# A transpose moved ahead of two weight transfers, and three fill steps moved across a score block: softcap attention followed by a maxout layer on one core

## The chip, the core and the metric

The kernel runs on one core of a Trainium2 chip. The metric is the device time of one execution in microseconds (us). Five engines of the core work side by side, each through its own queue of instructions in order: TensorE (PE in the profile, its weight loads apart as PEld), VectorE (DVE), ScalarE (ACT), GpSimd (POOL) and SyncE (SP). SP computes nothing here; it issues DMA transfers. The engines wait for one another through semaphores.

## The reference

For 8 batches of 12 heads, with 448 positions and a head size of 64, the reference computes softcap attention, and then feeds the result as 3584 rows of 768 numbers to a layer with two hidden products:

```
scores = (q @ k.T) / 8
scores = 30 * tanh(scores / 30)
attn   = exp(scores) / sum(exp(scores))        # the maximum is subtracted first
x      = attn @ v                              # 3584 x 768 after the heads are joined
out    = maximum(x @ w1, x @ w2) @ w_out       # w1, w2: 768 x 1024; w_out: 1024 x 768
```

The kernel doesn't subtract the maximum, since the cap bounds the scores. It uses maximum(a, b) = relu(a - b) + b: with wd = w1 - w2 it forms relu(x @ wd) @ w_out + x @ (w2 @ w_out). So w1 - w2 has to be computed once (`wd_sb`), and w2 @ w_out once (`wm_sb`).

## The kernel before

**Tiling.** Two heads make a pair, and there are N = 48 pairs. Three pairs are a group (g = 0 to 15, L = 3), the unit of loading. Two pairs are a quad (t = 0 to 23), the unit of attention. Pair i = 2t + p belongs to group i // 3. So quad 2 uses pairs 4 and 5 (group 1), quad 3 uses pairs 6 and 7 (group 2), quad 4 uses pair 8 (group 2) and pair 9 (group 3), and quad 5 uses pairs 10 and 11 (group 3).

**From q and k to scores.** For each group SP loads k and q (`load`, lines 117 to 145) into `kr` and `qr`; GpSimd casts them to bf16 into `kqf` (`cast`, lines 147 to 197; the last instruction of a cast of q is at line 190); then k and q must be turned so that the head dimension lies on the partitions. Pairs 0 to 5 are turned on TensorE. From group 2 on, `cross(g, n0, n1)` (line 290, its instruction at line 292) issues a DMA transpose of pairs n0 to n1 of the group on SP's queue, from `kqf` to `qkT`. `scores(t, p, last, js)` (line 302) multiplies for one pair: for each of three j two matmuls (line 318) into one PSUM tile, and then one tanh on ScalarE (line 319). The PSUM tiles are `s` (two buffers) or, where `last` is `v_psum` and for the last j, `v` (one buffer). `scores(t, 2)` does the 64 left-over keys of both pairs (line 315). `ex` is the exponential on ScalarE (line 324).

**Sums, values, the layer.** `total(t)` sums the exponentials on TensorE (lines 358, 362, 365), `values(t)` multiplies by v (lines 381, 387), and `normalize` scales on VectorE (line 402) into `xT`. When all quads of a batch are done, the layer for it (`moe`, line 406) is put into a list of fill work, `fill_q`: products with `wd_sb` (line 414), relu on VectorE (line 419), products with `wm_sb` (line 431) and `w_out` (line 434), copies (line 437) and stores. Ahead of these, the list holds the work that makes `wm_sb` (`turn_w2`, line 240; `premultiply`, line 249). `F(n)` (line 462) issues about n matmuls from the list, times `rate[0]`, which is 0.94 for quads 3 to 5 and 1.0 otherwise; a fraction left over is carried on. So the order of all work on every engine is written out by hand, with `F(n)` between the pieces of attention.

**wd_sb.** `load_w1(c, part)` (line 228, its instruction at line 232) loads half a block of 128 rows of w1 on SP's queue, 256 KB. Blocks 0 to 3 go to the `osb` buffers, blocks 4 and 5 to an `xT` buffer. `subtract(c, part, eng)` (line 234, its instruction at line 236) makes the block of `wd_sb`. Part 0 of blocks 0 and 1 and part 1 of block 5 are subtracted on VectorE, the rest on GpSimd. Part 0 serves the first four blocks of the hidden dimension, part 1 the last four.

**The stretch around the change.** Between lines 580 and 632 the program issues, on SP's queue: w1 part 0 of blocks 0 and 1, the transpose of the first pair of group 2 (pair 6), w1 part 0 of blocks 2 and 3, the main loads of k and q of pair 8, the transpose of pair 7, w1 part 0 of blocks 4 and 5, loads of group 3, the transpose of pair 8, w1 part 1 of all blocks, the transpose of pair 9 (`cross(3, 0, 1)`), loads for groups 3, 2 and 4, and the transpose of pairs 10 and 11 (`cross(3, 1, 3)`). A transpose waits on SP until the cast of its pair is done, and everything behind it in the queue waits with it. On GpSimd, in this order: the casts of pairs 6 and 7, half of a v cast, the subtractions of blocks 2 and 3 (part 0), the cast of pair 8, the subtractions of blocks 4 and 5 (part 0), the cast of pair 9, the subtractions of blocks 0 to 4 (part 1), and the casts of pairs 10 and 11.

The loop over the quads from 3 on (line 652) emits, for quad t, the scores of quad t + 1: `scores(t+1, 0, v_psum)` first, `scores(t+1, 1, v_psum)` in the middle (line 675), `scores(t+1, 2)` near the end, with `F(n)` and the additions of the exponentials on VectorE (`add`) between.

Of the kernel before, what the change touches and what calls it, by code (L numbers as in the profile page):

```python
# [10 lines left out]
def kernel(  # L11
# [216 lines left out]
    def load_w1(c, part):  # L228
        if c not in w1_in:
            w1_in[c] = opool.tile([P, DF], f32, name="osb") if c < OB else w1x[:, (c - OB) * DF : (c - OB + 1) * DF]  # L230
        cs = slice(part * (DF // 2), (part + 1) * (DF // 2))
        nc.sync.dma_start(out=w1_in[c][:, cs], in_=x_rows(moe_w1, c)[:, cs])

    def subtract(c, part, eng):
        cs = slice(part * (DF // 2), (part + 1) * (DF // 2))
        eng.tensor_sub(wd_sb[:, c, cs], w1_in[c][:, cs], w2b[part][:, c, :])
# [31 lines left out]
    def qkT_of(g):  # L268
        if g not in qkT:
            qkT[g] = stage.tile([P, L, 8, P], bf16, name="qkT")  # L270
        return qkT[g]
# [18 lines left out]
    def cross(g, n0=0, n1=L):  # L290

        nc.sync.dma_start_transpose(
            out=qkT_of(g)[:, n0:n1].rearrange("p n j c -> p (n j) c"),
            in_=kqf[g % 2][:, n0:n1].rearrange("p n j c -> p (n j c)"),
        )
# [6 lines left out]
    def scores(t, p, last=None, js=None):  # L302

        if (t, p) not in tanh:
            tanh[t, p] = att.tile([P, 2 * NJ, S], bf16, name="tanh")
        for j in js or range(NJ if p < 2 else 1):
            s = two_banks(last if last and j == NJ - 1 else s_psum)
            for m in range(2):
                i = 2 * t + (p if p < 2 else m)
                g = i // L  # L310
                k0 = qkT[g][:, i % L, :, :].rearrange("p j c -> p (j c)")
                o = Q0 + (64 * (i // NP % 2) if g >= NT else 0)
                qTn = k0[:, o : o + S]
                if p == 2:
                    nc.tensor.matmul(s[:, m, :S], k0[:, 3 * P : 4 * P], qTn)  # L315
                else:
                    r = slice(64 * m, 64 * m + 64)
                    nc.tensor.matmul(s[:, m, :S], k0[r, j * P : (j + 1) * P], qTn[r, :])  # L318
            nc.scalar.activation(tanh[t, p][:, 2 * j : 2 * j + 2, :], s[:, :, :S], AF.Tanh, scale=scale / cap)  # L319

    def ex(t, p):
        n = 2 * NJ if p < 2 else 2
        expo[t, p] = att.tile([P, n, S], bf16, name=f"expo{p}", bufs=2)
        nc.scalar.activation(expo[t, p], tanh[t, p][:, 0:n, :], AF.Exp, scale=float(cap))  # L324
# [6 lines left out]
    def add(t, ab, step):  # L331

        if t < NS or t >= NQ:
            return
        if t not in esum:
            esum[t] = att.tile([P, 4, S], bf16, name="esum")
        d = esum[t][:, 2 * ab : 2 * ab + 2, :]
        if step == 2:

            r = slice(64 * ab, 64 * ab + 64)  # L340
            d = esum[t][r, ab::2, :]
            nc.vector.tensor_add(d, d, expo[t, 2][r, :, :])  # L342
        elif step == 0:
            nc.vector.tensor_add(d, e_of(t, ab, 0), e_of(t, ab, 1))  # L344
        else:
            nc.vector.tensor_add(d, d, e_of(t, ab, 2))  # L346
# [5 lines left out]
    def total(t):  # L352

        ss = two_banks(s_psum)[:, 0, :]
        if t < NS:
            for j in range(NJ):
                for ab, h, r in HEADS:
                    nc.tensor.matmul(
                        ss[r, :S], ones[:, :32], e_of(t, ab, j)[:, h, :], start=(j == 0), stop=False
                    )  # L360
            for ab, h, r in HEADS:
                nc.tensor.matmul(ss[r, :S], ones2[:, h, :32], expo[t, 2][:, ab, :], start=False, stop=True)
        else:
            for ab, h, r in HEADS:
                nc.tensor.matmul(ss[r, :S], ones[:, :32], esum[t][:, 2 * ab + h, :], start=True, stop=True)  # L365
        st = att.tile([P, NB, 32], f32, name="st", bufs=1)
        nc.vector.transpose(st.rearrange("p b c -> p (b c)"), ss[:, :S])  # L367
        rs = att.tile([P, NB, 1], f32, name="rs", bufs=2)
        nc.vector.reciprocal(rs, st[:, :, 0:1])
        inv[t] = att.tile([P, S], f32, name="inv", bufs=2)  # L370
        nc.vector.transpose(inv[t].rearrange("p (b c) -> p b c", c=32), rs.to_broadcast([P, NB, 32]))  # L371

    def values(t):

        out = two_banks(v_psum)
        for u in range(2):
            ps = out[:, u, :]
            for j in range(NJ):
                for ab, h, r in HEADS:
                    g, n = divmod(2 * t + ab, L)  # L380
                    nc.tensor.matmul(  # L381
                        ps[r, :S], vp[g % 2][:, 2 * n + h, j, u::2], e_of(t, ab, j)[:, h, :],
                        start=(j == 0), stop=False,
                    )
            for ab, h, r in HEADS:
                g, n = divmod(2 * t + ab, L)
                nc.tensor.matmul(  # L387
                    ps[r, :S], vl[g % 2][:, n, 64 * h + u : 64 * h + 64 : 2], expo[t, 2][:, ab, :], start=False, stop=True
                )
        return out  # L390
# [9 lines left out]
    def normalize(t, ps):  # L400
        for u in range(2):
            nc.vector.tensor_mul(x_of(t, u), ps[:, u, :S], inv[t])  # L402
# [59 lines left out]
    def F(n):  # L462
        rate[1] += n * rate[0]
        while rate[1] >= 1 and fill_q:
            g = fill_q[0]
            if g is not rate[2]:
                rate[2] = g
                next(g)
            rate[1] -= 1
            try:  # L470
                next(g)
            except StopIteration:
                fill_q.pop(0)
        if not fill_q:
            rate[1] = 0.0
# [20 lines left out]
    def extra(i):  # L496
        for f, a in todo[i]:
            f(*a)
# [48 lines left out]
    def load_mains(g, n0, n1):  # L547
        for what in ("k", "q"):
            load(g, what, n0, n1, ("main",))
# [30 lines left out]
    for c in range(2):  # L580
        load_w1(c, 0)
    cross(2, 0, 1)
    for c in range(2, 4):
        load_w1(c, 0)
    load_mains(2, 2, 3)
    cross(2, 1, 2)
    for c in range(4, KC):
        load_w1(c, 0)
    load_mains(3, 0, 1)
# [62 lines left out]
    for t in range(3, NQ):  # L652
        i = 2 * t
        more = t + 1 < NQ
        rate[0] = 0.94 if t < 6 else 1.0
        if more:
            scores(t + 1, 0, v_psum)
        ex(t, 2)
        F(6)
        if t in crosses:  # L660
            cross(crosses[t])
        if t == 3:
            cast(nc.gpsimd, 3, "v")
        extra(i)
        F(2)
        add(t, 0, 0)
        F(3)
        if t == 3:
            subtract(5, 1, nc.vector)
        add(t, 0, 1)  # L670
        F(3)
        add(t, 1, 0)
        F(2)
        if more:
            scores(t + 1, 1, v_psum)
            ex(t + 1, 0)
        F(3)
        add(t, 1, 1)
        F(7)
        add(t, 0, 2)  # L680
        F(4)
        add(t, 1, 2)
        extra(i + 1)
        F(8)
        if more:
            scores(t + 1, 2)
            ex(t + 1, 1)
        total(t)
        normalize(t, values(t))
        if casts[t]:  # L690
            nc.gpsimd.tensor_copy(mark, inv[t][:1, :1])  # L691
            for g, what in casts[t]:
                cast(nc.gpsimd, g, what)
        if t % 3 == 2:
            fill_q.append(moe(t // 3))
        F(9)
# [34 lines left out]
```

## Time and profile before

The three runs of the kernel took 339.49, 339.53 and 340.0 us, a median of 339.53 us. The profiled execution has a span of 338.1 us.

| what | value |
|---|---|
| PE busy | 323.7 us (96% of the span) |
| ACT busy | 278.1 us (82%) |
| DVE busy | 229.0 us (68%) |
| POOL busy | 114.3 us (34%) |
| DMA moved | 61.78 MB, 183 GB/s on average |
| chain that ended last, by engine | PE 78%, DMA 12%, DVE 3%, ACT 3% |
| granted TensorE clock | full over the whole span |

How to read it: busy times are of one execution, and the engines overlap. The chain that ended last is followed back from the last instruction, at each step to whatever released it. A table of waits names for each waiting instruction what came last of the things it waited for. The timeline gives start and duration of each instruction, several of one kind merged (x4), and in brackets how long its engine sat idle before it and what ended that. For a DMA the duration in the timeline is that of its issue on SP's queue; when it landed is told apart. PE's ends are modelled, so merged neighbours can overlap by a tenth of a microsecond or two. Times below count from the start of the span.

### The profile page before, as it was taken

How to read it: one execution, taken by the hardware profiler on the slowest of the kernel's cores; microseconds unless marked ns; L12 is line 12 of the kernel's file. 1: busy time of each engine (PE TensorE's matmuls, PEld its weight loads, DVE VectorE, ACT ScalarE, POOL GpSimd, SP SyncE). 2: the span in 40 equal slices, each digit the busy share in tenths (PEclk: the TensorE clock that was granted, in tenths of full speed). 3: DMA queues.
4: the chain of work that ended last, by engine and by line, in shares of the span. 5: the costliest groups of instructions: out<-in, count | busy, mean ns of one | idle time of the engine just before them, and what ended most of it. 6: DMA issues, size and time to landing. Idle time of an engine off the chain costs nothing.

```text
span 338.1 us, 6876 instructions
## 1 busy us (share of the span) xinstructions
PE 323.7 (96%) x2721; PEld 163.8 (48%) x2722; DVE 229.0 (68%) x414; ACT 278.1 (82%) x243; POOL 114.3 (34%) x196
## 2 busy tenths in 40 slices
PE   4899989999999999999999999999999999999995
PEld 2555434455445454455445544445444554555563
DVE  4446865678787767768787576876886687874411
ACT  4999989999999999899989998999989999800000
POOL 8344698554323431440341344044034220000000
PEclk9999999999999999999999999999999999999999
DMA  7999999999997699568939699849955820012032
GB/s 221 188 237 280 264 241 293 261 257 237 214 311 156 189 233 282 134 158 188 315 96 221 87 263 292 176 100 240 295 107 137 211 95 2 0 48 93 2 93 93
DMA packets 106239, 61.78 MB, mean 183 GB/s; under 512 B 62816, under 2 KB 101088, under 8 KB 106208
## 3 DMA queue, kind: packets, MB, share of 16 engines
q1 hardware_dynamic: 102336, 58.21, 67.2%
q0 software_dynamic: 3872, 3.15, 6.1%
q8 instruction: 21, 0.34, 0.4%
q14 instruction: 10, 0.08, 0.1%
HBM read 42.47 MB, written 11.01 MB: 158 GB/s over the span
## 4 chain that ended last, share of the span: by engine, by line
PE 78%; DMA 12%; DVE 3%; ACT 3%; POOL 1%; issue 1%; SPq 1%; POOLq 0%; DVEq 0%
PE mm L434 22%; PE mm L414 20%; PE mm L431 16%; PE v L381 6%; PE s L318 6%; DMA kr<-in_k_dram 5%; DMA qkT<-kqf 3%; DMA kr<-in_moe_w_out_dram 2%; PE v L318 2%; DMA gT<-in_moe_w_dram 2%; PE v L387 2%; PE s L315 2%; PE s L365 2%; ACT expo L324 1%; ACT tanh L319 1%
## 5 line engine op out<-in xcount | busy, mean ns | idle before, releaser
L324 ACT ACTIVATE expo<-tanh 128x2688 bf16<-128x2688 bf16 (+1 forms) x72 | 140.3, 1950 | 0.2
L319 ACT ACTIVATE tanh<-s 128x896 bf16<-128x896 f32 x123 | 107.4, 915 | 13.7 <-PE s L318 11.0
L434 PE MATMUL mm<-wo_sb,gT 128*128 128x384 bf16 (+2 forms) x448 | 86.3, 327 | 0.0
L414 PE MATMUL mm<-xT,wd_sb 128*128 128x448 bf16 x384 | 78.4, 353 | 0.9 <-DVE gT L419 0.6
L431 PE MATMUL mm<-wm_sb,xT 128*128 128x384 bf16 (+2 forms) x335 | 65.5, 326 | 0.1
L437 DVE COPY osb<-mm 128x384 f32<-128x384 f32 (+2 forms) x56 | 31.1, 556 | 43.4 <-PE mm L434 42.8
L434 PEld LDWEIGHTS <-gT 128*128 128x128 bf16 x448 | 41.9, 98 | 35.9 <-issue 9.9
L414 PEld LDWEIGHTS <-wd_sb 128*128 128x128 bf16 x384 | 35.7, 98 | 40.4 <-issue 9.9
L419 DVE TENSOR_SCALAR gT<-mm 128x448 bf16<-128x448 f32 x64 | 39.6, 622 | 20.9 <-PE mm L414 18.4
L691 POOL COPY mark<-inv 1x1 f32<-1x1 f32 x17 | 3.0, 177 | 124.8 <-DVE inv L371 109.0
L431 PEld LDWEIGHTS <-xT 128*128 128x128 bf16 x336 | 32.0, 98 | 24.7 <-issue 4.1
L319 ACT ACTIVATE tanh<-v 128x896 bf16<-128x896 f32 x45 | 41.6, 925 | 0.0
L381 PE MATMUL v<-expo,vp 128*32 128x448 bf16 x576 | 35.9, 353 | 0.0
L318 PE MATMUL s<-qkT 64*128 64x448 bf16 x198 | 28.3, 363 | 3.6 <-DVE qkT L288 1.8
L402 DVE TENSOR_TENSOR xT<-v,inv 128x448 bf16<-128x448 f32 x48 | 27.7, 620 | 2.6 <-PE v L387 0.3
L346 DVE TENSOR_TENSOR esum<-esum,expo 128x896 bf16<-128x896 bf16 x40 | 26.9, 672 | 1.0
L367 DVE STREAM_TRANSPOSE st<-s 128x448 f32<-128x448 f32 x24 | 15.6, 648 | 16.7 <-PE s L365 12.7
L342 DVE TENSOR_TENSOR esum<-esum,expo 64x896 bf16<-64x896 bf16 x40 | 25.0, 625 | 1.2
L344 DVE TENSOR_TENSOR esum<-expo 128x896 bf16<-128x896 bf16 x40 | 25.8, 645 | 0.0
L318 PEld LDWEIGHTS <-qkT 64*128 64x128 bf16 x288 | 10.5, 95 | 25.7 <-issue 15.6
L381 PEld LDWEIGHTS <-vp 128*32 128x32 bf16 x576 | 15.8, 97 | 10.0 <-DVE vp L157 0.4
L185 POOL CAST kqf<-qr 128x1152 bf16<-128x1152 f32 (+2 forms) x17 | 17.0, 999 | 6.7 <-DMA qr<-in_q_dram 5.8
(68 smaller groups left out, 266.2 us busy)
## 6 DMA issues: line engine op xcount, KB each, us to landing
vr<-in_v_dram SPq DMA_DIRECT2D x14, 576.0 KB, 5.0
out_dram<-osb SPq DMA_DIRECT2D x20, 384.0 KB, 3.9
kr<-in_k_dram SPq DMA_DIRECT2D x12, 576.0 KB, 6.6
qr<-in_q_dram SPq DMA_DIRECT2D x12, 576.0 KB, 7.1
out_dram<-osb SPq DMA_DIRECT2D x14, 192.0 KB, 4.7
osb<-in_moe_w_dram SPq DMA_DIRECT2D x8, 256.0 KB, 4.2
gT<-in_moe_w_dram POOLq DMA_DIRECT2D x12, 128.0 KB, 9.4
wo_sb<-in_moe_w_out_dram POOLq DMA_DIRECT2D x4, 384.0 KB, 8.6
```

What stands on the lines that cost most here:

```text
L318: nc.tensor.matmul(s[:, m, :S], k0[r, j * P : (j + 1) * P], qTn[r, :])
L319: nc.scalar.activation(tanh[t, p][:, 2 * j : 2 * j + 2, :], s[:, :, :S], AF.Tanh, scale=scale / cap)
L324: nc.scalar.activation(expo[t, p], tanh[t, p][:, 0:n, :], AF.Exp, scale=float(cap))
L344: nc.vector.tensor_add(d, e_of(t, ab, 0), e_of(t, ab, 1))
L346: nc.vector.tensor_add(d, d, e_of(t, ab, 2))
L381: nc.tensor.matmul(ps[r, :S], vp[g % 2][:, 2 * n + h, j, u::2], e_of(t, ab, j)[:, h, :], start=(j == 0), stop=False,)
L402: nc.vector.tensor_mul(x_of(t, u), ps[:, u, :S], inv[t])
L414: nc.tensor.matmul(ps[:, :S], wd_sb[:, c, f * P : (f + 1) * P], x[:, c, cs], start=(c == 0), stop=(c == KC - 1))
L419: nc.vector.tensor_relu(g[f // FH][:, f % FH, cs], ps[:, :S])
L431: nc.tensor.matmul(ps, x[:, c, ts], wm_sb[:, c, hs], start=(c == 0), stop=False)
L434: nc.tensor.matmul(ps, g[f // FH][:, f % FH, ts], wo_sb[:, f, hs], start=False, stop=(f == FC - 1))
L437: nc.vector.tensor_copy(osb[:, hs], ps)
```

## The change

```diff
     for c in range(2):
         load_w1(c, 0)
     cross(2, 0, 1)
+    cross(2, 1, 2)
     for c in range(2, 4):
         load_w1(c, 0)
     load_mains(2, 2, 3)
-    cross(2, 1, 2)
     for c in range(4, KC):
         load_w1(c, 0)
     load_mains(3, 0, 1)
...
         add(t, 1, 0)
-        F(2)
+        F(2 if t > 3 else 5)
         if more:
             scores(t + 1, 1, v_psum)
             ex(t + 1, 0)
         F(3)
         add(t, 1, 1)
-        F(7)
+        F(7 if t > 3 else 4)
         add(t, 0, 2)
```

The first part moves the transpose of pair 7 on SP's queue: it is issued directly behind the transpose of pair 6, ahead of w1 part 0 of blocks 2 and 3 and of the main loads of pair 8, which each move one place back. It is meant to bring pair 7 to TensorE sooner. The second part concerns quad 3 alone, which is the fourth: three units of fill work are taken from behind the scores of pair 9 and put ahead of them. With the rate of 0.94 these are two matmuls in the instruction stream: two products of line 414 stand ahead of the six score matmuls of pair 9 that stood behind them. Nothing is added or removed: all engines have the same instructions as before, GpSimd in the same order.

## The prediction

> **What bounds the kernel now.** I read first the page's busy times, then the busy time by stretch, to find where TensorE has idle time at all, then TensorE's waits, then the timelines of the engines around the edit.
>
> Page, busy time by engine:
>
> ```profile
> PE 323.7 (96%) x2721; PEld 163.8 (48%) x2722; DVE 229.0 (68%) x414; ACT 278.1 (82%) x243; POOL 114.3 (34%) x196
> ```
>
> Busy time by stretch (start:end, length, then busy us of PE, PEld, DVE, ACT, POOL; clock, DMA share, GB/s):
>
> ```profile
> 46.00:67.00 21.00, 20.15 (x182) 9.38 (x180) 11.98 (x22) 19.28 (x16) 16.42 (x24) 1.00 1.03 256
> 67.00:130.00 63.00, 62.73 (x508) 31.04 (x509) 47.12 (x81) 61.51 (x55) 24.77 (x37) 1.00 0.94 231
> 130.00:330.00 200.00, 199.32 (x1567) 100.37 (x1567) 140.73 (x250) 157.43 (x137) 45.73 (x76) 1.00 0.59 150
> ```
>
> From 67 us to 330 us TensorE idles 0.27 + 0.68 = 0.95 us in all. Its work there is fixed, so the end is (the moment at which TensorE gets to its work of 67 us) + (a constant). Before that it has waits. Table of TensorE's waits from 30 us on (total, times, longest):
>
> ```profile
> PE s L318 <- DMA qkT<-kqf: 1.8, 2, 1.4
> PE mm L414 <- DVE gT L419: 0.6, 1, 0.6
> PE v L318 <- ACT tanh L319: 0.4, 1, 0.4
> ```
>
> The largest are two waits for a DMA transpose. TensorE's timeline says where:
>
> ```profile
> 44.96 0.55 PE L318 MATMUL s<-qkT 64*128 64x448 bf16 x4 [1.35 <-DMA qkT<-kqf]
> ...
> 57.92 0.37 PE L318 MATMUL v<-qkT 64*128 64x448 bf16 x2 [0.43 <-ACT tanh L319]
> ...
> 67.01 0.55 PE L318 MATMUL s<-qkT 64*128 64x448 bf16 x4 [0.42 <-DMA qkT<-kqf]
> ```
>
> By program order these are the scores of pair 7 (44.96, the transpose that the edit moves), of pair 9 (56.94, its third part 57.92) and of pair 10 (67.01, the transpose of pairs 10 and 11). The edit aims at the first. The question is whether the last one lets any of it through. SP's timeline shows the issues (start, duration of the issue):
>
> ```profile
> 35.49 2.20 SPq L292 DMA_TRANSPOSE qkT<-kqf  x1
> 37.74 1.04 SPq L232 DMA_DIRECT2D osb<-in_moe_w_dram  x2
> ...
> 39.87 1.34 SPq L292 DMA_TRANSPOSE qkT<-kqf  x1
> ...
> 46.31 1.26 SPq L292 DMA_TRANSPOSE qkT<-kqf  x1
> 47.62 2.86 SPq L232 DMA_DIRECT2D osb<-in_moe_w_dram  x4
> ...
> 60.72 3.12 SPq L292 DMA_TRANSPOSE qkT<-kqf  x1
> ```
>
> and GpSimd's timeline shows who waits for these:
>
> ```profile
> 41.35 2.27 POOL L236 TENSOR_TENSOR wd_sb<-osb,gT 128x512 bf16<-128x512 f32 x2 [2.00 <-DMA osb<-in_moe_w_dram]
> ...
> 45.99 0.29 POOL L190 CAST kqf<-qr 64x128 bf16<-64x128 f32 x1
> ...
> 51.85 4.49 POOL L236 TENSOR_TENSOR wd_sb<-osb,gT 128x512 bf16<-128x512 f32 x4 [1.38 <-DMA osb<-in_moe_w_dram]
> ...
> 60.30 0.40 POOL L190 CAST kqf<-qr 64x256 bf16<-64x256 f32 x1
> ```
>
> The reader is to see one chain through these rows. w1 part 0 of block 2, issued at 37.74, lands 3.5 us later (41.24); GpSimd, idle for 2.00 us, starts its subtractions at 41.35; behind them stands the cast of pair 8, done at 45.99 + 0.29 = 46.28; SP issues that transpose at 46.31 (its queue had been ready since 45.65); behind it stands w1 part 1, issued at 47.62, landing 4.1 us later; GpSimd, idle for 1.38 us, starts at 51.85, ends the casts of pairs 10 and 11 at 60.70; SP issues their transpose at 60.72; it lands 6.24 us later, at 66.96; TensorE starts pair 10 at 67.01. **The moment that sets the end hangs on the landing of w1 block 2**, and this is what the edit moves back.
>
> **The Trainium skill.** "DMA: Bandwidth & Descriptors", section "Queues, rings and completion order": SP owns one row of rings, and on each DMA engine descriptors are consumed in ring order. So what is issued first from SP is moved first; the trace fits: w1 block 2 landed at 41.24, behind the first transpose (35.49 + 4.3 = 39.8). "SBUF — State Buffer", section "Who interferes with whom": a VectorE instruction with two SBUF inputs and a GpSimd instruction that reads SBUF exclude each other. The trace agrees: VectorE's subtraction takes 0.70 us at 44.57 and 1.23 at 42.94 beside GpSimd's, and GpSimd's cast of k takes 0.50 us at 48.58 and 0.96 at 43.58. "TensorE: Matmul & The Clock Gate", "The mechanism": matmuls start and end in strict order; so fill behind waiting scores can't run, as the idle 1.35 us shows.
>
> **The change part by part.**
>
> *The transpose of pair 7 moves ahead.* Its cast ended at 37.42 and SP was free at 37.69, so it can issue at 37.74 instead of 39.87. The first transpose landed 4.3 us after its issue, the old place gave 5.04, and the third, on a quiet queue, 3.2. Thus it lands at 41 to 42.8. TensorE wants it at 44.96 - 1.35 = 43.61. I take the whole 1.35 us as gone, at this place.
>
> *Who profits.* ScalarE doesn't at first: the tanh of pair 7 started at 45.58, right behind an exponential that ended at 45.55, so PSUM tiles come free no sooner than 46.5, and `total(2)`, at 47.50 before, can't start before that. So 1.0 us of the 1.35 goes on, and ScalarE's wait for TensorE at 48.77 (1.47 us) shrinks by as much. On this side quad 3 runs 1.0 us ahead.
>
> *w1 blocks 2 and 3 and the loads of pair 8 move back* by one issue of a transpose. Transposes of one pair took 1.34, 1.26 and 1.29 us (the last at 51.59), and the first of all took 2.20. I take 1.3, with 2.2 as the upper bound. w1 block 2 then issues at 39.05; with the same 3.5 us behind a transpose in flight it lands at 42.55. GpSimd starts at 42.65 in place of 41.35. Queued behind the waiting subtraction are all casts of pairs 8 to 11. From 41.35 to 46.28 GpSimd needed 4.93 us, of which 2.27 (subtractions) + 1.9 (four casts, as at 48.58 to 50.47) = 4.17 is its own and 0.76 is exclusion by VectorE. VectorE's two subtractions stay near 43 to 45 us, so they still meet GpSimd. I take no recovery; a full one is the lower bound, 1.3 - 0.76 = 0.5. The loads of pair 8 move from 38.83 to about 40.15 and land 3.7 us later, before GpSimd wants them at 44.9: nothing.
>
> *On from there*, 1.3 us later all along: cast of pair 8 done 47.6 (SP waits longer in its place), w1 part 1 issued 48.9, subtractions from 53.15, casts of pairs 10 and 11 done 62.0, transpose issued 62.0, landed 68.25. The slack that the trace shows on the way (GpSimd's idle 1.38 us, SP's wait ahead of 60.72) is not slack of this chain: both wait for members of it. The loads of k and q for pairs 10 and 11 are issued at 52.92 and 54.04 in the same queue behind w1 part 1, so they shift too.
>
> *The fill moved ahead.* Pair 9's transpose was issued at 51.59 and took 5.0 us (56.6); now about 57.9. TensorE would be there at 56.94 - 1.0 = 55.9, with two products at 0.2 us each at 56.3. The two products cost nothing: they lie in this wait of 1.6 us. So TensorE starts pair 9 at 57.9, about 1 us later than before, and its lead is gone. Then it needs block 4 of `wd_sb` part 1, ready 57.96 + 1.3 = 59.3, for the second product behind the scores: some 0.4 us of wait. It reaches pair 10 at about 67.3, and waits for 68.25.
>
> *Sum.* Gone: 1.35 us at 44.96. New: 1.6 at pair 9, 0.4 at the product, and about 1.0 in place of 0.42 at pair 10. The start of pair 10 moves from 67.01 to 68.3, +1.3 us, and after that nothing is left to make it up. 339.5 + 1.3 = 340.8 us. By the bounds: +0.5 gives 340.0, +2.2 gives 341.7.
>
> **The rivals.**
>
> *No change (339.5).* w1 block 2 lands nearly as early, or the exclusion of GpSimd is gone by the shift, and pair 10's transpose lands where it did. For it: 0.76 us of exclusion that can vanish, and the DMA queue was held back by the 2.20 us issue at 35.49. Against: even then at least 0.5 us is left, by my count. TensorE's gain of 1.0 us ends in the wait at 67.
>
> *Faster.* The chain through GpSimd doesn't shift, and pair 10's transpose lands sooner than in 6.24 us (pair 9's took 5.0, pair 8's 3.2). Then up to the 1.0 us that passes ScalarE comes through: 339.5 - 1.0 = 338.5. For it: the 6.24 us are mostly queueing behind the v and k loads, which can fall otherwise. Against: those loads shift with the chain, and GpSimd waits for w1 at 41.35 with nothing between.
>
> *Slower by more.* The second transpose also takes 2.2 us to issue, back to back with the first: 341.7. This is the upper end of the likeliest case.
>
> **How the numbers follow.** The shifted chain: 0.62, of which a little falls under 0.2% (0.68 us), but some of the case of no change lies above it too. No change: 0.2. Faster: 0.18. So faster 0.19, same 0.21, slower 0.6. The range goes from 338.8, which leaves out the outer part of the faster case, to 341.8, the 2.2 us bound.
>
> **What would show it.** Right: TensorE's wait at pair 7 gone; the second transpose issued near 37.7; GpSimd's first w1 subtraction near 42.6 instead of 41.35; pair 8's transpose near 47.6; the transpose of pairs 10 and 11 near 62.0, and pair 10 on TensorE near 68.3, with a longer wait for the DMA. Wrong: GpSimd starting its subtractions before 41.9, or its cast of pair 8 ending by 46.3; or the transpose of pairs 10 and 11 landing before 66.9.

## The result, and the profile after

The changed kernel took 341.74 us (median of 6 runs, 340.36 to 342.63), beside 339.51 us of the kernel before (6 runs, 338.98 to 340.0): ratio 1.0062, 95% interval 1.0036 to 1.0087. It is slower by 2.2 us. The forecast was 340.8 us with a range up to 341.8. The views below are those shown of before, of an execution of the changed kernel with a span of 340.4 us and a time of 342.32 us.

The page, busy time by engine:

```profile
PE 323.8 (95%) x2722; PEld 163.5 (48%) x2722; DVE 229.8 (67%) x414; ACT 277.9 (82%) x243; POOL 114.0 (33%) x196
```

All engines do the same work as before. Busy time by stretch (start:end, length, busy us of PE, PEld, DVE, ACT, POOL; clock, DMA share, GB/s):

```profile
28.00:46.00 18.00, 17.42 (x207) 8.68 (x205) 15.08 (x26) 16.78 (x17) 12.00 (x23) 1.00 1.05 262
46.00:67.00 21.00, 18.89 (x174) 8.71 (x173) 11.25 (x20) 19.66 (x16) 17.17 (x28) 1.00 1.12 246
67.00:130.00 63.00, 61.12 (x499) 30.24 (x498) 46.39 (x79) 59.14 (x53) 24.46 (x37) 1.00 0.94 227
130.00:330.00 200.00, 199.37 (x1569) 99.94 (x1568) 141.90 (x252) 159.82 (x139) 46.36 (x79) 1.00 0.60 153
```

The stretches up to 46 us, first of the kernel before, then of the changed one:

```profile
0.00:28.00 28.00, 21.18 (x245) 12.39 (x246) 13.52 (x36) 23.34 (x21) 14.36 (x33) 1.00 1.08 225
28.00:46.00 18.00, 16.12 (x199) 8.31 (x198) 14.28 (x26) 16.54 (x17) 13.01 (x27) 1.00 1.06 270
...
0.00:28.00 28.00, 20.39 (x242) 12.18 (x243) 13.13 (x35) 22.55 (x21) 13.99 (x33) 1.00 1.07 223
```

The gain that was aimed at is there, but it is small: from 28 to 46 us TensorE is busy 1.30 us more than before (17.42, 16.12), and 0.79 us of this is work that this execution hadn't done yet at 28 us (20.39, 21.18). Some 0.5 us remain. From 46 to 67 us it does 1.26 us less than before (18.89, 20.15), and the next row loses 1.61 us more, since pair 10 now falls into it. After that nothing differs. TensorE's largest waits (total, times, longest), and where they are:

```profile
PE s L318 <- DMA qkT<-kqf: 1.6, 1, 1.6
PE s L318 <- ACT expo L324: 1.3, 1, 1.3
```

```profile
43.68 0.36 PE L318 MATMUL s<-qkT 64*128 64x448 bf16 x2
44.33 0.36 PE L318 MATMUL s<-qkT 64*128 64x448 bf16 x2 [0.28 <-ACT tanh L319]
...
58.15 0.55 PE L318 MATMUL s<-qkT 64*128 64x448 bf16 x4 [1.34 <-ACT expo L324]
...
64.31 0.75 PE L381 MATMUL v<-expo,vp 128*32 128x448 bf16 x12 [0.60 <-POOL vp L164]
...
69.40 0.55 PE L318 MATMUL s<-qkT 64*128 64x448 bf16 x4 [1.62 <-DMA qkT<-kqf]
```

Pair 7 (43.68, its second two matmuls at 44.33) no longer waits for its transpose. Pair 9 (58.15) and pair 10 (69.40) do. The wait at 58.15 is put down to an exponential of ScalarE, but SP issued that transpose at 52.92 and it landed 5.2 us later, at 58.1: the transpose was the real release. SP's timeline (start, duration of the issue):

```profile
34.67 1.34 SPq L292 DMA_TRANSPOSE qkT<-kqf  x1
36.63 2.40 SPq L292 DMA_TRANSPOSE qkT<-kqf  x1
39.08 1.06 SPq L232 DMA_DIRECT2D osb<-in_moe_w_dram  x2
...
44.47 0.61 SPq L136 DMA_DIRECT2D qr<-in_q_dram  x1
47.50 1.26 SPq L292 DMA_TRANSPOSE qkT<-kqf  x1
48.81 2.99 SPq L232 DMA_DIRECT2D osb<-in_moe_w_dram  x4
...
62.54 3.03 SPq L292 DMA_TRANSPOSE qkT<-kqf  x1
```

and GpSimd's:

```profile
42.45 2.72 POOL L236 TENSOR_TENSOR wd_sb<-osb,gT 128x512 bf16<-128x512 f32 x2 [3.76 <-DMA osb<-in_moe_w_dram]
...
47.18 0.29 POOL L190 CAST kqf<-qr 64x128 bf16<-64x128 f32 x1
...
52.96 4.49 POOL L236 TENSOR_TENSOR wd_sb<-osb,gT 128x512 bf16<-128x512 f32 x4 [1.28 <-DMA osb<-in_moe_w_dram]
...
59.76 0.82 POOL L185 CAST kqf<-kr 128x768 bf16<-128x768 f32 x1 [0.74 <-DMA kr<-in_k_dram]
```

The reader is to see the same chain as before, each link later: w1 issued at 39.08 (37.74 before), GpSimd at 42.45 (41.35), the transpose of pair 8 at 47.50 (46.31), GpSimd's second batch at 52.96 (51.85), the transpose of pairs 10 and 11 at 62.54 (60.72), pair 10 at 69.40 (67.01). From 45.08 to 47.50 SP's queue stands still, 2.42 us in place of 0.66. Behind that hole the DMA engines move less: in the row for 47 to 51 us (last two numbers: DMA share, GB/s) they moved 100 GB/s, and 211 in the same row of the kernel before, which stands second:

```profile
47.00:51.00 4.00, 4.00 (x58) 1.90 (x58) 2.68 (x6) 3.48 (x3) 3.73 (x8) 1.00 1.08 100
...
47.00:51.00 4.00, 4.00 (x58) 1.71 (x57) 2.61 (x6) 2.53 (x3) 3.29 (x7) 1.00 0.94 211
```

The share of 1.08 shows that the engines weren't empty over these 4 us. Only from 48 to 49 us is it low (0.37 at 73 GB/s; 1.30 at 215 before). From 49 to 51 us it is 1.61 at 106 GB/s, while the transpose of pair 8 was on its way; it landed 4.5 us after its issue (3.2 before).

### The profile page after: what moved, and what is told of

It is laid out like the page before. It is cut to its first block, busy times and chain, and to the rows that moved or that the text cites. A ratio compares the mean times of both kernels' runs of the same rounds, so it can differ in the third digit from the quotient of the medians.

```text
span 340.4 us, 6877 instructions
## 1 busy us (share of the span) xinstructions
PE 323.8 (95%) x2722; PEld 163.5 (48%) x2722; DVE 229.8 (67%) x414; ACT 277.9 (82%) x243; POOL 114.0 (33%) x196
## 4 chain that ended last, share of the span: by engine, by line
PE 75%; DMA 16%; DVE 3%; SPq 2%; POOL 2%; issue 1%; POOLq 0%; DVEq 0%
PE mm L434 21%; PE mm L414 19%; PE mm L431 16%; PE v L381 6%; PE s L318 5%; DMA qr<-in_q_dram 3%; DMA vr<-in_v_dram 3%; DMA gT<-in_moe_w_dram 2%; PE v L387 2%; PE v L318 2%; DMA kr<-in_moe_w_out_dram 2%; DMA qkT<-kqf 2%; PE s L315 2%; DMA xT<-in_moe_w_dram 2%; PE s L365 2%; DMA osb<-in_moe_w_dram 1%
```

## The experiments

The theory is the chain: the landing of w1 block 2, GpSimd's queue, SP's queue, the transpose of pairs 10 and 11, pair 10 on TensorE. The rivals: the moved fill costs the time; two transposes back to back cost it; or where w1 stands doesn't matter. The kernel before ran beside each experiment, with medians of 339.94 to 340.43 us, so ratios are compared.

**The two parts of the change, each alone.** The transpose moved, the fill as before:

> The transpose of pair 7 moved ahead as in the changed kernel, the fill left where it was. Theory (chain through the landing of w1 block 2 on GpSimd): the two products of fill lay in a wait, so this costs as much as the whole change: 341.7 us, pair 10 on TensorE near 69.4. Rival (the fill put ahead of pair 9 is what costs): 339.5 us or less.

Measured: 341.36 us, ratio 1.0046 (1.0030 to 1.0061). In the profiled execution pair 10 started at 67.96, not near 69.4. The fill moved, the transpose as before:

```diff
-        F(2)
+        F(2 if t > 3 else 5)
...
-        F(7)
+        F(7 if t > 3 else 4)
```

> The fill moved as in the changed kernel, the transpose left where it was. Theory: TensorE comes to pair 9 some 0.4 us later and loses its 0.43 us wait for the tanh there; it still waits for the transpose of pairs 10 and 11: 339.5 us (339.2 to 339.8). Rival (the fill is what costs): 341 us or more.

Measured: 339.94 us, ratio 0.9996 (0.9982 to 1.0009); the kernel before took 339.94 us beside it, so the window was missed by 0.1 us with no difference behind it. The fill does nothing that can be measured, and the moved transpose alone is slower. The intervals of the transpose alone and of the whole change overlap, so no difference between these two is shown. TensorE's timeline of the fill alone carries a second reading:

```profile
43.10 0.83 PE L318 MATMUL s<-qkT 64*128 64x448 bf16 x4
...
67.08 0.55 PE L318 MATMUL s<-qkT 64*128 64x448 bf16 x4 [1.67 <-DMA qkT<-kqf]
```

Here SP's queue has the old order, and pair 7 (43.10) doesn't wait at all. The 1.35 us at which the change aimed was that of one execution.

**w1 delayed alone.** The kernel before, with the two w1 parts one place back, behind the loads of pair 8. No transposes are adjacent, and pair 8's loads come earlier:

```diff
     cross(2, 0, 1)
+    load_mains(2, 2, 3)
     for c in range(2, 4):
         load_w1(c, 0)
-    load_mains(2, 2, 3)
     cross(2, 1, 2)
```

> The kernel before, with w1 blocks 2 and 3 put behind the two main loads of pair 8; the transpose of pair 7 keeps its place, no two transposes are adjacent, the fill is as before. w1 is issued some 0.95 us later. Theory: GpSimd's first subtraction near 42.3 in place of 41.35, pair 10's transpose issued 1 to 1.7 us later, the end at 340.5 to 341.5 us, with the wait of 1.35 us at pair 7 still there. Rival (adjacent transposes or fill cost the time): 339.5 us.

Measured: 341.60 us, ratio 1.0049 (1.0028 to 1.0069). The delay of w1 alone is enough (the time is 0.1 us above its window). SP's timeline and GpSimd's:

```profile
43.62 0.61 SPq L136 DMA_DIRECT2D qr<-in_q_dram  x1
46.65 1.26 SPq L292 DMA_TRANSPOSE qkT<-kqf  x1
...
61.63 2.97 SPq L292 DMA_TRANSPOSE qkT<-kqf  x1
```

```profile
41.59 2.72 POOL L236 TENSOR_TENSOR wd_sb<-osb,gT 128x512 bf16<-128x512 f32 x2 [3.27 <-DMA osb<-in_moe_w_dram]
```

The mark is the idle time of GpSimd, 3.27 us for w1, and SP's hole from 44.23 to 46.65, 2.42 us, as in the changed kernel. Two details missed: the wait at pair 7 was 0.22 us, not 1.35, and GpSimd's first subtraction started at 41.59, not near 42.3. Both are matters of the single execution, in which SP reached the transpose of pair 6 1.05 us sooner than in that of the kernel before (34.44, 35.49).

**More of the delay.** The changed kernel, w1 behind the loads of pair 8:

```diff
     cross(2, 0, 1)
     cross(2, 1, 2)
+    load_mains(2, 2, 3)
     for c in range(2, 4):
         load_w1(c, 0)
-    load_mains(2, 2, 3)
```

> The changed kernel, with w1 blocks 2 and 3 one place further back, behind the main loads of pair 8: the suspected delay grows from 1.3 to about 2.25 us, the transposes are as in the changed kernel. Theory: the end another 0.9 to 1.5 us later, 342.5 to 343.3 us. Rival (the adjacency of the transposes costs, not w1): 341.7 us as the changed kernel.

Measured: 344.33 us, ratio 1.0124 (1.0099 to 1.0149): 4.2 us above the kernel before, more than forecast. SP's timeline has the hole grown to 5.04 us (44.78 to 49.82):

```profile
44.18 0.60 SPq L136 DMA_DIRECT2D qr<-in_q_dram  x1
49.82 1.26 SPq L292 DMA_TRANSPOSE qkT<-kqf  x1
```

and GpSimd's has two waits for w1 instead of one:

```profile
44.30 1.16 POOL L236 TENSOR_TENSOR wd_sb<-osb,gT 128x512 bf16<-128x512 f32 x1 [5.31 <-DMA osb<-in_moe_w_dram]
46.79 1.16 POOL L236 TENSOR_TENSOR wd_sb<-osb,gT 128x512 bf16<-128x512 f32 x1 [1.33 <-DMA osb<-in_moe_w_dram]
```

The transposes stand as in the changed kernel, so the further delay of w1 costs time. The size has a second possible source: in this run the granted clock (third number from the end) fell to half for 3.4 us, as it does nowhere ahead of the last matmul in the profile of the changed kernel:

```profile
60.10:63.50 3.40, 3.18 (x12) 1.13 (x13) 1.76 (x3) 2.53 (x4) 1.89 (x5) 0.50 1.10 326
...
70.70 0.55 PE L318 MATMUL s<-qkT 64*128 64x448 bf16 x4 [0.23 <-DMA qkT<-kqf]
```

In this execution pair 10 still waited 0.23 us for its transpose, so the chain set its start. All six executions have a lower mean clock (0.988 to 0.995); how much that adds in the other five isn't shown.

**w1 ahead.** The changed kernel with w1 ahead of both transposes; then with the loads of pair 8 ahead too; and the kernel before with w1 ahead, the loads between the transposes:

```diff
+    for c in range(2, 4):
+        load_w1(c, 0)
     cross(2, 0, 1)
     cross(2, 1, 2)
-    for c in range(2, 4):
-        load_w1(c, 0)
     load_mains(2, 2, 3)
```

> The changed kernel, with w1 blocks 2 and 3 ahead of both transposes, which stay back to back. The loads then fall in the time in which SP waits for the cast of pair 6. Theory: GpSimd's first subtraction starts near 39.5 to 40 in place of 42.45, the casts and transposes behind it come 1 to 2 us earlier than in the kernel before, and the end at 338.0 to 339.5 us. Rival (two transposes back to back hold up the DMA queue and cost the time themselves): 341 us or more.

> The changed kernel, with both w1 blocks 2 and 3 and the main loads of pair 8 ahead of the two transposes, which stay back to back. In the run with w1 alone ahead, GpSimd then waited 1.42 us for the load of k of pair 8. Theory (whatever GpSimd's casts of pair 8 wait for last sets the chain): GpSimd waits for neither, the cast of pair 8 ends some 1.5 us earlier than in the run with w1 alone ahead, and the end is at 338.5 to 340.0 us, below that run's 340.75. Rival (two transposes back to back cost time themselves): still 340.7 us or more.

> The kernel before, with w1 blocks 2 and 3 ahead of the transpose of pair 6; the main loads of pair 8 stay between the two transposes, the fill is as before. Theory: GpSimd starts its subtractions near 39.6 and has the load of pair 8 as early as before, so the chain is some 1 us ahead of the kernel before: 338.5 to 339.5 us. Rival (the order of w1 doesn't matter when the transposes are apart): 339.9 us.

Measured: w1 alone ahead 340.75 us, ratio 1.0028 (1.0011 to 1.0045); w1 and k ahead 340.12, ratio 0.9999 (0.9979 to 1.0020); w1 ahead with the transposes apart 340.02, ratio 0.9996 (0.9982 to 1.0011). The first missed its expectation: it lies between the two kernels. GpSimd's timeline shows what took over:

```profile
39.60 2.29 POOL L236 TENSOR_TENSOR wd_sb<-osb,gT 128x512 bf16<-128x512 f32 x2 [0.60 <-DMA osb<-in_moe_w_dram]
43.30 0.72 POOL L185 CAST kqf<-kr 128x384 bf16<-128x384 f32 x1 [1.42 <-DMA kr<-in_k_dram]
```

The subtractions start 2.85 us earlier than in the changed kernel, but the cast of pair 8 then waits 1.42 us for k, which the change moves behind both transposes too. With k ahead as well, no cost of the two adjacent transposes is to be seen against the kernel before (the interval reaches up to 0.2%), and the delay of w1 alone costs time with none adjacent. So the loss doesn't need adjacency. But none of these kernels beats the kernel before, as the expectations had it (the last two miss theirs by 0.1 and 0.5 us): in these three profiled runs the transpose of pairs 10 and 11 is issued at 60.25 to 60.94 and pair 10 starts at 66.50 to 67.23, as before. The earlier links of the chain were ahead, its end wasn't. GpSimd began its second batch 1.3 to 1.9 us sooner (49.97 to 50.58, 51.85 before) and then stood once more within it, for 0.82 to 1.48 us, until a later block of w1 part 1 had landed. So these loads took most of the lead back.

**SP's queue kept going.** w1 part 1 ahead of the transpose of pair 8, in the changed kernel and in the kernel before:

```diff
-    cross(2, 2, 3)
     for c in range(KC):
         load_w1(c, 1)
+    cross(2, 2, 3)
```

> The changed kernel, with w1 part 1 of all blocks issued ahead of the transpose of pair 8 instead of behind it, so that SP's queue doesn't stand still while GpSimd is late with the cast of pair 8 (in the changed kernel it stood from 45.08 to 47.50). Theory (the loss is the time in which SP's queue stands still and the DMA engines run empty): the loss goes, 339.3 to 340.3 us. Rival (GpSimd's lateness itself sets pair 10, wherever the loads stand): still 341.2 us or more.

> The kernel before, with the same move of w1 part 1 ahead of the transpose of pair 8. SP stood still for only 0.66 us there. Theory: a gain of at most that, 339.2 to 340.0 us beside 339.9 of the kernel before. Rival (the order costs time elsewhere: pair 8's transpose is now some 3 us later than TensorE wants it): 341 us or more.

Measured: 340.69 us, ratio 1.0024 (1.0004 to 1.0043), in the changed kernel; 340.52, ratio 1.0011 (0.9993 to 1.0029), in the kernel before. The second misses its window by 0.5 us and shows no gain. The first misses its own by 0.4 us: the point is more than half of the loss lower, but its interval touches that of the changed kernel. The move opens a wait of its own, in TensorE's timeline of the first, and behind this wait the granted clock fell to half for 3.4 us:

```profile
55.09 0.55 PE L318 MATMUL s<-qkT 64*128 64x448 bf16 x4 [2.66 <-DMA qkT<-kqf]
...
55.80 4.99 PE L414 MATMUL mm<-xT,wd_sb 128*128 128x448 bf16 x17
...
55.70:59.10 3.40, 3.40 (x11) 1.35 (x10) 0.72 (x2) 3.23 (x4) 1.92 (x3) 0.50 0.95 295
```

Pair 8's transpose now comes late itself (2.66 us; 1.77 in the other). The 17 products behind it took 4.99 us, where 17 took 3.39 in the changed kernel. In this execution the transpose of pairs 10 and 11, issued at 61.53, landed 4.4 us later, and pair 10 started only at 69.32: TensorE itself was late. Such executions are the smaller part: 4 of the 22 have a mean clock of 0.989 to 0.993 and took 342.21 to 344.15 us, and the median of the others is 340.53 us. In the other kernel they are 5 of 22 (0.992 to 0.994, 341.61 to 342.25 us), and the median of the others is 340.22 us. So some executions of these two kernels lose time in a way that none of the six of the changed kernel shows (mean clock 0.998 and above). They don't tell how much of its loss is the hole in the queue and how much GpSimd's lateness.

**The casts ahead on GpSimd.** The changed kernel, SP untouched:

```diff
+    cast_kq(2, 2, 3)
     for c in range(2, 4):
         subtract(c, 0, nc.gpsimd)
-    cast_kq(2, 2, 3)
-    for c in range(4, KC):
-        subtract(c, 0, nc.gpsimd)
...
     cast_kq(3, 0, 1)
+    for c in range(4, KC):
+        subtract(c, 0, nc.gpsimd)
```

> The changed kernel, SP's queue untouched, but on GpSimd the cast of pair 8 stands ahead of the subtractions of blocks 2 and 3, and the cast of pair 9 ahead of those of blocks 4 and 5. So the casts no longer queue behind the landing of w1 blocks 2 and 3. Theory (the order on GpSimd is what ties pair 8's transpose to w1): SP stands still less than 1.2 us ahead of that transpose, in place of 2.42, and most of the loss goes: 339.6 to 340.6 us beside about 340.0 of the kernel before; a TensorE wait of up to 1 us for blocks 4 and 5 of the difference may show near 52 us. Rival (the later issue of the loads alone costs, whatever GpSimd does): 341.2 us or more.

Measured: 340.95 us, ratio 1.0013 (0.9988 to 1.0037). That is inconclusive: the interval takes in no change and reaches into that of the changed kernel. The profile contradicts the expected 1.2 us: SP still stood for 2.01 us (44.84 to 46.85), since the cast, freed from w1, waited for k:

```profile
44.27 0.83 POOL L185 CAST kqf<-kr 128x384 bf16<-128x384 f32 x1 [5.31 <-DMA kr<-in_k_dram]
```

TensorE also waited twice for blocks of the difference, 0.86 and 0.75 us, where up to 1 us was expected. Either load that the change moves back can hold the cast of pair 8: w1 does in the changed kernel, k does here.

**Fill put into the last wait.** Six units of fill ahead of pair 10, in both kernels:

```diff
         ex(t, 2)
-        F(6)
+        F(6 if t != 4 else 0)
...
-        F(9)
+        F(9 if t != 3 else 15)
     F(10 ** 9)
```

> The changed kernel, with the six units of fill work behind the first scores of pair 10 put ahead of them, where TensorE waited 1.62 us for the transpose. Theory (TensorE's work behind that point is fixed and it alone sets the end): some 1.1 us of the wait are used, 340.5 to 340.9 us. Rival (ScalarE, which starts pair 10 with its tanh, sets the end, and the time at which pair 10 starts is what counts): 341.7 us.

> The kernel before, with the same six units of fill ahead of pair 10, where TensorE waited 0.42 us in the profiled run. Theory: the wait is used, 339.3 to 339.7 us beside 339.9. Rival (ScalarE sets the end): 339.9 to 340.6 us, since pair 10 starts later.

Measured: 341.33 us, ratio 1.0052 (1.0033 to 1.0072), and 339.81, ratio 0.9996 (0.9980 to 1.0012). Neither can be told from the kernel that it was made of. The gain of 1.1 us in the first isn't shown; by the table below, the time from the start of pair 10 to the end is only some 0.2 us shorter than in the kernel that each was made of, so most of the moved work can't be seen there. Why isn't known.

**One table over all profiled runs.** For each: how long SP's queue stood ahead of pair 8's transpose (end of the issue before it to its start), when pair 10 started on TensorE, span, time of that execution. The two runs with w1 part 1 ahead are left out, since their order is another there (SP stood 0.26 and 0.10 us, pair 10 started at 69.32 and 67.49, and the first is the one in which TensorE itself was late).

| kernel | SP stood | pair 10 | span | us |
|---|---|---|---|---|
| w1 and k ahead | 0.10 | 67.23 | 338.5 | 340.29 |
| w1 ahead, apart | 0.11 | 66.51 | 338.0 | 339.94 |
| fill alone | 0.57 | 67.08 | 338.3 | 340.35 |
| w1 ahead | 0.58 | 66.50 | 338.0 | 339.90 |
| before | 0.66 | 67.01 | 338.1 | 340.05 |
| before, fill in the last wait | 1.75 | 69.17 | 340.0 | 341.82 |
| transpose alone | 2.01 | 67.96 | 339.7 | 341.56 |
| casts ahead | 2.01 | 68.09 | 339.4 | 341.45 |
| w1 delayed alone | 2.42 | 68.58 | 339.9 | 341.88 |
| changed | 2.42 | 69.40 | 340.4 | 342.32 |
| changed, fill in the last wait | 2.42 | 70.22 | 341.1 | 343.10 |
| w1 delayed more | 5.04 | 70.70 | 342.1 | 343.93 |

Span minus start of pair 10 is 271.0 to 271.7 us in every row without fill ahead of it (and 270.8 and 270.9 with): the end is set when pair 10 starts. And the time doesn't depend on the standing time up to 0.66 us and is above all of these from 1.75 us on. This is a relation over single executions, not an experiment of its own.

## Why the prediction was right, and where its size was off

**The end is the start of pair 10 plus a constant.** Right: 338.1 - 67.01 = 271.1 before, 340.4 - 69.40 = 271.0 after.

**The wait at pair 7 goes, and ScalarE lets only part of it on.** Right in kind: it went, a wait of 0.28 us for a tanh came, and the next idle time of ScalarE fell from 1.47 to 0.52 us. The lead was smaller, though: ScalarE was itself 0.37 us later in this execution (tanh of pair 7 at 45.95, 45.58 before), and TensorE came to `total(2)` 0.58 us sooner (46.92, 47.50 before), not 1.0. The wait at pair 9 swallows this either way.

**w1, GpSimd, SP up to the second batch.** Right to within 0.2 us in this execution: w1 issued at 39.08 (39.05 forecast), GpSimd at 42.45 (42.65), no recovery from the exclusion (5.02 us up to the end of pair 8's cast, 4.93 before), pair 8's transpose at 47.50 (47.6), w1 part 1 at 48.81 (48.9), GpSimd's second batch at 52.96 (53.15). That it fits so closely is luck in part. The forecast of 39.05 was 35.49 with issues of 2.20 and 1.3 behind it. What came was another sum: SP reached its first transpose 0.82 us sooner (34.67), issued it in 1.34 us, stood 0.62 us until the cast of pair 7 was done, and then took 2.40 us for the second. And the start of the forecast was that of one execution: in the three other profiled runs with w1 right behind the first transpose (fill alone; before with w1 part 1 ahead; before with fill in the last wait) w1 was issued at 35.69 to 36.67 and landed 4.0 to 5.7 us later, not at 37.74 and 3.5 us later. What holds over executions is GpSimd's start on w1: 40.31 to 42.05 in these three and the kernel before, 41.74 to 42.67 in four with the changed order (changed; transpose alone; w1 part 1 ahead; fill in the last wait). The means are 1.1 us apart, and the ranges overlap.

**The last links.** Here 1.1 us was missed in this execution: pair 10 at 69.40, not 68.3. The step that was mis-sized is "1.3 us later all along": it took the durations of the loads and of the transpose at the end of the chain as fixed. Measured: GpSimd waited 0.74 us for k of pairs 10 and 11, which landed 5.4 us after its issue at 54.20 (4.9 before); so their casts ended at 62.51 in place of 62.0. Then their transpose landed 6.81 us after its issue (6.24 before). 0.5 + 0.6 = 1.1 us. That these two are slower because of the hole in SP's queue isn't shown, and other runs speak against it: the fill alone, with SP standing 0.57 us, has 5.9 and 6.8 us for them, and the transpose alone, with 2.01 us, has 5.3 and 6.2 and pair 10 at 67.96, ahead of the forecast. Nor is the miss clear of the noise: the interval of the ratio is 1.2 to 3.0 us, and the forecast of 1.3 us lies just within it.

**Pair 9 and the fill.** Pair 9 at 58.15 (57.9 forecast) with 1.34 us of wait (1.6), and the fill alone at no cost: right. The wait of 0.4 us for block 4 of the difference didn't come. One of 0.60 us for a cast of v did, unforeseen; it lies ahead of the wait at pair 10, which would have been that much longer.

**The rivals.** "No change" rested on w1 landing nearly as early: it didn't. "Faster" needed pair 10's transpose to land sooner: it landed later. The bound "slower by more" (341.7) comes nearest to the measured 341.74. Its reason holds in part: the second transpose did take 2.40 us to issue, but the first only 1.34, with 0.62 us of standing between them.

What stays open: how much of the 2.2 us is SP's hole and how much GpSimd's lateness, how much of the time with w1 delayed more is the clock's, and why w1 alone ahead stayed 0.28% above the kernel before while its profiled execution didn't.

## What to carry to other kernels

When a transfer is moved up a queue, ask who waits for what it passes: here a cast on another engine stood behind two loads of 256 KB, the next transfer of the same queue waited for that cast, and the kernel became 2.2 us slower, while the wait that was removed was worth nothing because the same chain set a later one. Count a wait as a prize only if it shows in several executions and no later wait for the same chain takes it back. And a load that is on the chain when it is late need not gain anything when it is early: here the loads behind it set the pace then.

## What the runs showed of the hardware that was not expected

The issue of a transpose of one pair on SP's queue mostly took 1.2 to 1.5 us, but in a quarter of the cases 1.7 to 3.8 us. It isn't tied to a place: that of pair 6 took 2.20 us before and 1.34 in the changed kernel, that of pair 7 took 2.40 in the changed kernel, 1.25 with the transpose alone, 1.45 with w1 delayed more and 3.19 with w1 and k ahead.

With the old order of the transposes, the wait at pair 7 was 1.35 us in the kernel before, 0.22 with w1 delayed alone, 0.45 with fill in the last wait, and none for the transpose in the two others (fill alone; w1 part 1 ahead). The first issue of a transpose, 2.20 us in the profile before, took 1.34 in these four.

In two profiled runs the granted TensorE clock fell to half for 3.4 us, near the end of a wait of TensorE for a transpose: of 1.89 us (w1 delayed more; from 60.1 us) and of 2.66 us (w1 part 1 ahead in the changed kernel; from 55.7 us). A wait of 1.91 us at the same place in another run (changed, fill in the last wait) went by with the full clock. Whether the wait brings the fall about isn't shown.

In the run of the kernel before with six units of fill put ahead of pair 10, SP stood 1.75 us although its queue had the old order: w1 block 2 reached GpSimd only at 42.05. So the old order has the late landing too; how often, single profiles don't tell. The times of the kernel before in these series spread from 338.47 to 342.65 us.
